# Transposing the softmax probabilities as 4-byte words of two keys in a cached attention kernel

## The chip, the cores and the metric

The kernel runs on one core of a Trainium2 chip. The metric is the device time of one execution in microseconds. Before the change, three runs took 957.71, 957.88 and 958.71 us, so the median is 957.88 us.

## The reference

There are two independent attention blocks, A and B, with weights and caches of their own. All inputs are bf16. For one block:

```python
B, Sq, D = 16, 64, 640
H, Sk, Dh = 32, 512, 128
q = (x @ wq).reshape(B, Sq, H, Dh).transpose(0, 2, 1, 3)
scores = einsum("bhqd,bhkd->bhqk", q, k_cache) * Dh ** -0.5
p = softmax(scores, axis=-1)
o = einsum("bhqk,bhkd->bhqd", p, v_cache)
out = o.transpose(0, 2, 1, 3).reshape(B, Sq, H * Dh) @ wo
```

The two outputs, each 16 x 64 x 640, are concatenated along the last axis. For each block, batch and head, the caches hold 512 keys and values of 128 numbers.

## The kernel before

**Tiling.** Two batches of 64 queries each share the 128 partitions. A *step* is one head of such a pair of batches, and a *macro step* `m` is two neighbouring heads (called `sub` 0 and 1 below). A pass goes through half of the heads (16) of one block for all eight pairs of batches. That makes 4 passes, 32 groups of 8 macro steps, and 256 macro steps in all. In a group the output projection is accumulated in PSUM over 16 heads. The first half's sum is parked in SBUF in f32 (OVP, ScalarE), and the second half's is added to it and stored (OVF, VectorE, then ST, a DMA that ScalarE issues).

**One macro step**, by the names in the code and the lines of the profile:

- KX (L433, TensorE): eight transposes of 128x128 blocks of K for one batch of the pair, into the one PSUM bank `KT_BANK`. KE (L442, VectorE) copies the bank to `ktp_ring`. Each is done twice a macro step, as KX0, KE0, KX1, KE1, and all four use the same bank.
- QP2 (L451, TensorE): the query projection, ten matmuls. QE2 (L459, ScalarE) copies it out with the scale.
- SM2 (L467, TensorE): the scores, four matmuls of 64 queries by 512 keys; two at a time share the array by its column halves.
- MX (L476, VectorE): the row maximum. EX (L482, ScalarE): the exponential, with the row sum. RC2 (L488, VectorE): the reciprocal of the sums.
- NM (L496, GpSimd): P times the reciprocal, one instruction per head, from `p_ring` to `pn_ring`. It also puts the keys in another order, described below.
- TR2 (L505, TensorE): eight transposes of 128x128 blocks of P into `PT_BANK`. The block of data is the weight load (stationary), and the identity is the moving operand. TE2 (L512, VectorE) copies the bank to `pT_ring`.
- PV2 (L524, TensorE): P times V, sixteen matmuls; a block of V is stationary, and 64 columns of `pT_ring` move. OE2 (L532, ScalarE) copies it out.
- OP2 (L540, L545, TensorE): the output projection, a matmul of 512 columns and one of 128 for each head.
- Once a group: XT (L604, TensorE) and XE (L612, ScalarE) transpose x for the projection, through `PT_BANK` too.

**Order.** Each engine runs a fixed list. Templates give an engine's order within one turn of the loop, and the number behind a name says how many macro steps ahead it works:

```python
PE_T = (("TR2", 1), ("QP2", 4), ("KX", 4, 0), ("SM2", 3), ("PV2", 1), ("XT", 0), ("OP2", 0), ("KX", 4, 1))
ACT_T = (("QE2", 4), ("OE2", 1), ("XE", 0), ("EX", 3, 0), ("EX", 3, 1), ("OV", 0), ("ST", -1))
DVE_T = (("TE2", 1), ("RC2", 2), ("KE", 4, 0), ("MX", 3, 0), ("MX", 3, 1), ("KE", 4, 1), ("OVF", 0))
POOL_T = (("NM", 0, 0), ("NM", 0, 1))
```

So on TensorE a turn goes TR2, QP2, KX0, SM2, PV2, (XT), OP2, KX1, and then the next turn's TR2. Semaphore waits are worked out from reads and writes of the buffers (`build_plan`, `prune_waits`), and the first instruction of an operation carries the wait. SyncE issues all loads by a plan with due times: K and V come in chunks of four heads into rings of five.

**The order of the keys.** V lies with key 4p + t on partition p in slot t. K's partitions hold eight neighbouring keys each, so the transposed K, the scores and P have their 512 keys in the order (key mod 8, key div 8): position 64 i + pp is key 8 pp + i. For PV2 the transposed P must have keys 4p + t on partition p, so NM writes its result permuted: with i = 4 th + tl, the key goes to place 128 tl + 2 pp + th.

Of the kernel before, what the change touches and what calls it, by code (L numbers as in the profile page):

```python
# [14 lines left out]
class Cfg:  # L15
    G = 4
    HH = 16
    NKB = 5
# [46 lines left out]
def build_plan(dims, cfg):  # L65
# [32 lines left out]
    def make_op(kind, m, sub):  # L98
        g0, g1 = 2 * m, 2 * m + 1
        ps_, bp, grp, h0 = step_info(g0)  # L100
        c = g0 // G
        if kind == "KX":
            return mk("pe", "KX", (m, sub), [("kn", c % cfg.NKB, g0 % G), ("kn", c % cfg.NKB, g1 % G), ("ident",)],
                      [("KTB",)], "KX%d" % sub, m, sub)
        if kind == "KE":
            return mk("dve", "KE", (m, sub), [], [("KTB",), ("ktp", m % cfg.NKT, sub)], "KE%d" % sub, m, sub)
        if kind in ("MX", "EX", "NM"):
            g = 2 * m + sub
            r = g % cfg.NR
            if kind == "MX":  # L110
                return mk("dve", "MX", g, [], [("SB", sub), ("negmax", r)], "MX%d" % sub, m, sub)
            if kind == "EX":
                return mk("act", "EX", g, [("negmax", r)], [("SB", sub), ("p", g % cfg.NP), ("rowsum", r)],
                          "EX%d" % sub, m, sub)
            return mk("pool", "NM", g, [("p", g % cfg.NP), ("recip", r)], [("pn", g % cfg.NPN)], "NM%d" % sub, m, sub)
        r0, r1 = g0 % cfg.NR, g1 % cfg.NR
        if kind in ("XT", "XE"):
            mt = m + cfg.XLEAD
            if mt % MPG != 0 or not (0 <= mt < NMAC):
                return None  # L120
            gq = mt // MPG
            m_ts = mt - cfg.XLEAD + OFF["TR2"]
            if kind == "XT":
                return mk("pe", "XT", gq, [("xn", gq % cfg.NXN), ("ident",)], [("PTB",)], "XT", m_ts, aux=gq)
            return mk("act", "XE", gq, [], [("PTB",), ("xT", gq % cfg.NX)], "XE", m_ts, aux=gq)
        if kind == "QP2":
            return mk("pe", "QP2", m, [("xT", grp % cfg.NX), ("wq", ps_ % 2, h0 // G)], [("QB",)], "QP2", m)
        if kind == "QE2":
            return mk("act", "QE2", m, [], [("QB",), ("qT", m % cfg.NQ)], "QE2", m)
        if kind == "SM2":  # L130
            return mk("pe", "SM2", m, [("qT", m % cfg.NQ), ("ktp", m % cfg.NKT, 0), ("ktp", m % cfg.NKT, 1)],
                      [("SB", 0), ("SB", 1)], "SM2", m)
        if kind == "RC2":
            return mk("dve", "RC2", m, [("rowsum", r0), ("rowsum", r1)], [("recip", r0), ("recip", r1)], "RC2", m)
        if kind == "TR2":
            return mk("pe", "TR2", m, [("pn", g0 % cfg.NPN), ("pn", g1 % cfg.NPN), ("ident",)], [("PTB",)], "TR2", m)
        if kind == "TE2":
            return mk("dve", "TE2", m, [], [("PTB",), ("pT", m % cfg.NT)], "TE2", m)
        if kind == "PV2":
            return mk("pe", "PV2", m, [("pT", m % cfg.NT), ("v", c % cfg.NVB, g0 % G), ("v", c % cfg.NVB, g1 % G)],  # L140
                      [("OB",)], "PV2", m)
        if kind == "OE2":
            return mk("act", "OE2", m, [], [("OB",), ("oT", m % cfg.NO)], "OE2", m)
        if kind == "OP2":
            return mk("pe", "OP2", m, [("oT", m % cfg.NO), ("wo", ps_ % 2, h0 // G)], [("OUTB",)], "OP2", m)
        if kind in ("OV", "OVF", "ST"):
            if h0 + 1 != SPB - 1:
                return None
            last_half = ps_ % NHALF == NHALF - 1
            if kind == "OV":  # L150
                if NHALF == 1:
                    return mk("act", "OV", m, [], [("OUTB",), ("out_sb", grp % 2)], "OV", m, aux=grp)
                if last_half:
                    return None
                return mk("act", "OVP", m, [], [("OUTB",), ("outp", bp)], "OV", m, aux=grp)
            if kind == "OVF":
                if NHALF == 1 or not last_half:
                    return None
                return mk("dve", "OVF", m, [("outp", bp)], [("OUTB",), ("out_sb", grp % 2)], "OV", m, aux=grp)
            if NHALF == 1 or not last_half:  # L160
                return None
            return mk("act", "ST", m, [("out_sb", grp % 2)], [("out_dram", grp)], "ST", m, aux=grp)
        raise ValueError(kind)

    templates = {"pe": cfg.PE_T, "dve": cfg.DVE_T, "pool": cfg.POOL_T, "act": cfg.ACT_T}
    for eng, tmpl in templates.items():
        offs = [t[1] for t in tmpl] + [cfg.XLEAD]
        for k in range(-max(offs), NMAC - min(offs)):
            for t in tmpl:
# [8 lines left out]
                if 0 <= m < NMAC:  # L178
                    op = make_op(kind, m, sub)
                    if op is not None:  # L180
                        progs[eng].append(op)
                        if op.kind == "OV":
                            progs[eng].append(mk("act", "ST", m, [("out_sb", op.aux % 2)], [("out_dram", op.aux)],
                                                 "ST", m, aux=op.aux))

    progs["pool"] = [mk("pool", "INIT1", -1, [], [("ones",)], "LDW", -10),
                     mk("pool", "INIT2", -1, [("ones",)], [("ident",)], "LDX", -10)] + progs["pool"]

    loads = []
    NEG = -10 ** 9  # L190
# [53 lines left out]
    def sem_key(op):  # L244
# [5 lines left out]
            return ("d_" + op.kind[2:].lower(), op.aux[0] % 2, op.aux[1])  # L250
        if op.kind == "ST":
            return ("d_out", op.aux % 2)
        if op.kind in ("INIT1", "INIT2"):
            return ("s_init",)
        return ("s_" + op.kind.lower(),)

# [90 lines left out]
def mha_kernel(nc, blocks, out, cfg=None):  # L347
# [30 lines left out]
    with contextlib.ExitStack() as es:  # L378
# [13 lines left out]
        qT_ring = sb("qT_ring", [128, NQ, 2, 128], BF16)  # L392
        p_ring = sb("p_ring", [128, NP, SK], BF16)
        pn_ring = sb("pn_ring", [128, NPN, SK], BF16)
        pT_ring = sb("pT_ring", [128, NT, 2, 4, 128], BF16)
        oT_ring = sb("oT_ring", [128, NO, 2, 128], BF16)
        out_sb = sb("out_sb", [128, 2, DN], BF16)
        negmax = sb("negmax", [128, NR], F32)
        rowsum = sb("rowsum", [128, NR], F32)
        recip = sb("recip", [128, NR], F32)  # L400
        ones_sb = sb("ones_sb", [128, 128], BF16)
        ident = sb("ident", [128, 128], BF16)
        ps = es.enter_context(nc.psum_tensor("ps", [128, 8, 512], F32))

        sems = {}
# [9 lines left out]
        S_BANK0 = 2  # L415
        PT_BANK, O_BANK, Q_BANK, KT_BANK = 4, 5, 6, 7
        pt_ps_flat = ps[:, PT_BANK, :].bitcast(BF16)
        pt_ps = pt_ps_flat.rearrange("p (s t q) -> p s t q", s=2, t=4)
        o_ps = ps[:, O_BANK, 0:256]
        q_ps = ps[:, Q_BANK, 0:256]  # L420
        kt_ps_flat = ps[:, KT_BANK, :].bitcast(BF16)
# [5 lines left out]
        def em_KX(e, op):  # L427
# [2 lines left out]
            c, hp = g0 // G, (g0 % G) // 2  # L430
            first = last = None
            for t8 in range(8):
                ins = e.transpose(kt_ps[:, t8, :], kn_ring[:, c % NKB, j, hp, t8, :], ident[:, :])  # L433
                first = first or ins
                last = ins
            return first, last
# [54 lines left out]
        def em_NM(e, op):  # L491
            g = op.idx
            r = g % NR
            src = p_ring[:, g % NP, :].rearrange("q (th tl pp) -> q th tl pp", th=2, tl=4)
            dst = pn_ring[:, g % NPN, :].rearrange("q (tl pp th) -> q th tl pp", tl=4, th=2)
            ins = e.tensor_scalar(dst, src, recip[:, r:r + 1], 1.0, ALU.mult, ALU.mult)  # L496
            return ins, ins

        def em_TR2(e, op):
            m = op.idx  # L500
            first = last = None
            for sub in range(2):
                g = 2 * m + sub
                for t in range(4):
                    ins = e.transpose(pt_ps[:, sub, t, :], pn_ring[:, g % NPN, t * 128:(t + 1) * 128], ident[:, :])  # L505
                    first = first or ins
                    last = ins
            return first, last

        def em_TE2(e, op):  # L510
            m = op.idx
            ins = e.tensor_copy(pT_ring[:, m % NT].rearrange("p s t q -> p (s t q)"), pt_ps_flat)  # L512
            return ins, ins

        def em_PV2(e, op):
            m = op.idx
            first = last = None
            for sub in range(2):
                g = 2 * m + sub
                c, gi = g // G, g % G  # L520
                for j in range(2):
                    for t in range(4):
                        col = sub * 128 + 64 * j
                        ins = e.matmul(o_ps[:, col:col + 64], v_ring[:, c % NVB, j, gi, t, :],  # L524
                                       pT_ring[:, m % NT, sub, t, 64 * j:64 * j + 64], start=(t == 0), stop=(t == 3))
                        first = first or ins
                        last = ins
            return first, last
# [18 lines left out]
            return first, last  # L547

        def em_OV(e, op):
            ins = e.activation(out_sb[:, op.aux % 2, :], out_ps_all, ACTF.Copy)  # L550
            return ins, ins

        def em_OVP(e, op):
# [3 lines left out]

        def em_OVF(e, op):
            blk, bp = grp_info(op.aux)
            ins = e.tensor_tensor(out_sb[:, op.aux % 2, :], out_ps_all, outp[:, bp, :], ALU.add)  # L560
            return ins, ins

        def em_ST(e, op):
            blk, bp = grp_info(op.aux)
            dst = out[2 * bp:2 * bp + 2, :, blk * DN:(blk + 1) * DN].rearrange("b q n -> (b q) n")
            ins = e.dma_start(dst, out_sb[:, op.aux % 2, :])
            return ins, ins

        def em_INIT1(e, op):
# [3 lines left out]
        def em_INIT2(e, op):  # L573
            ins = e.affine_select(ident[:, :], ones_sb[:, :], [[1, 128]], ALU.is_equal, 0.0, base=0,
                                  channel_multiplier=-1)
            return ins, ins

        def em_LDWQ(e, op):
# [37 lines left out]
        def em_LDKV(e, op):  # L616
# [6 lines left out]
            else:  # L623
# [4 lines left out]

        emitters = dict(KX=em_KX, KE=em_KE, QP2=em_QP2, QE2=em_QE2, SM2=em_SM2, MX=em_MX, EX=em_EX, RC2=em_RC2,
                        NM=em_NM, TR2=em_TR2, TE2=em_TE2, PV2=em_PV2, OE2=em_OE2, OP2=em_OP2, OV=em_OV,  # L630
                        OVP=em_OVP, OVF=em_OVF, ST=em_ST, XT=em_XT, XE=em_XE, INIT1=em_INIT1, INIT2=em_INIT2,
                        LDWQ=em_LDWQ, LDWO=em_LDWO, LDX=em_LDX, LDK=em_LDKV, LDV=em_LDKV)

        def run_program(e, prog, final_waits=()):
# [85 lines left out]
```

## Time and profile before

| | us |
|---|---|
| median of three runs | 957.88 |
| lowest, highest | 957.71, 958.71 |
| span of the profiled execution | 956.8 |
| TensorE busy (matmuls) | 919.4 |
| VectorE busy | 841.9 |
| ScalarE busy | 567.1 |
| GpSimd busy | 416.9 |

The profiled execution is one of its kind; its span runs from the first to the last recorded instruction. Its own time outside the span is not recorded, but the three runs are 0.9 to 1.9 us over its span, and the median is 1.1 over it. TensorE's granted clock is full from the first tenths of the span to the end (mean 0.998). DMA moves 299.5 MB, at 313 GB/s on average.

How to read it: busy time counts an instruction from start to end, and neighbouring instructions on one engine overlap, so the mean time of one matmul (219 ns for a 128x128 one) is longer than what it costs in a row of them. The chain of waits goes back from the last instruction and gives each stretch of time to one piece of work; there the overlap is taken out. "PE" is TensorE's matmuls, "PEld" its weight loads, "DVE" VectorE, "ACT" ScalarE, "POOL" GpSimd. The number after "L" is the line in the code. A shape such as `128*64 128x512` on a matmul is the stationary block (rows by columns) and then the moving operand; a name such as `ps<-ident,pn_ring` gives the output, the moving and the stationary operand.

### The profile page before, as it was taken

The page shows a single profiled execution, that of the slowest core. Times are in us where ns is not written, and L with a number is a line of the kernel's source. Part 1 is how long each engine was busy: PE and PEld are TensorE (multiplying, and loading weights), DVE is VectorE, ACT ScalarE, POOL GpSimd, SP SyncE. Part 2 cuts the span into 40 slices and gives each one's busy share as a digit, 9 for nine tenths or more (in the row PEclk, how much of TensorE's full clock was granted, in tenths as well). Part 3 has the DMA queues.
Part 4 walks back from the last instruction along what each step waited for, and adds up shares of the span by engine and source line. Part 5 has one row for each costly group of instructions (what it writes and reads, how often), then busy time and mean ns, then how long its engine had stood idle before and what let it go on. Part 6 is the DMA issues. An engine that isn't in the chain of part 4 may idle for free.

```text
span 956.8 us, 34351 instructions
## 1 busy us (share of the span) xinstructions
PE 919.4 (96%) x14755; PEld 733.5 (77%) x15008; DVE 841.9 (88%) x1552; ACT 567.1 (59%) x1585; POOL 416.9 (44%) x518
## 2 busy tenths in 40 slices
PE   4999999999999999999999999999999999999997
PEld 3877777778777777877777787777877778777775
DVE  2898899898899999899999899889899998999996
ACT  1666656666665565656566666666666656565654
POOL 0444444444444444444444444444444444444443
PEclk9999999999999999999999999999999999999999
DMA  9999999999999999888999999988888988899830
GB/s 315 364 365 364 351 365 367 365 368 351 338 337 337 343 330 315 299 292 305 322 332 352 326 353 327 306 294 296 302 305 288 308 301 297 295 297 314 295 124 15
DMA packets 230871, 299.51 MB, mean 313 GB/s; under 512 B 9536, under 2 KB 165184, under 8 KB 230720
## 3 DMA queue, kind: packets, MB, share of 16 engines
q1 hardware_dynamic: 228416, 294.69, 91.0%
q8 instruction: 118, 1.93, 0.8%
q10 hardware_dynamic: 2304, 2.62, 0.8%
q14 instruction: 33, 0.27, 0.1%
HBM read 294.65 MB, written 2.62 MB: 311 GB/s over the span
## 4 chain that ended last, share of the span: by engine, by line
PE 89%; DVE 4%; POOL 3%; issue 2%; SPq 1%; DMA 1%; POOLq 0%; DVEq 0%
PE ps L433 22%; PE ps L524 14%; PE ps L451 14%; PE ps L467 14%; PE ps L505 12%; PE ps L545 7%; PE ps L540 5%; POOL pn_ring L496 3%; DVE out_sb L560 1%; DVE ktp_ring L442 1%; DVE pT_ring L512 1%; PE ps L604 1%; DMA xn_ring<-in_A_x_dram 1%; SPq L626 1%; SPq L583 1%
## 5 line engine op out<-in xcount | busy, mean ns | idle before, releaser
L496 POOL TENSOR_SCALAR pn_ring<-p_ring,recip 128x512 bf16<-128x512 bf16 x512 | 416.3, 843 | 532.7 <-DVE recip L488 532.7
L442 DVE COPY ktp_ring<-ps 128x1024 bf16<-128x1024 bf16 x512 | 353.7, 691 | 105.3 <-PE ps L433 85.1
L482 ACT ACTIVATE p_ring<-ps,negmax 128x512 bf16<-128x512 f32 x512 | 345.6, 684 | 4.8 <-DVE negmax L476 4.8
L476 DVE TENSOR_REDUCE negmax<-ps 128x1 f32<-128x512 f32 x512 | 327.3, 681 | 0.4 <-PE ps L467 0.3
L433 PE MATMUL ps<-ident,kn_ring 128*128 128x128 bf16 x4096 | 314.6, 220 | 2.8 <-DMA kn_ring<-in_A_k_cache_dram 1.6
L532 ACT ACTIVATE oT_ring<-ps 128x256 bf16<-128x256 f32 x256 | 98.0, 383 | 306.0 <-PE ps L524 306.0
L433 PEld LDWEIGHTS ps<-ident,kn_ring 128*128 128x128 bf16 x4096 | 251.9, 98 | 34.2 <-DVE ktp_ring L442 2.6
L524 PEld LDWEIGHTS ps<-pT_ring,v_ring 128*128 128x128 bf16 x4096 | 133.5, 98 | 109.2 <-issue 100.0
L451 PE MATMUL ps<-xT_ring,wq_sb 128*128 128x128 bf16 x2560 | 186.4, 220 | 3.2 <-DMA wq_sb<-in_A_wq_dram 3.2
L512 DVE COPY pT_ring<-ps 128x1024 bf16<-128x1024 bf16 x256 | 174.5, 682 | 4.6 <-PE ps L505 3.8
L524 PE MATMUL ps<-pT_ring,v_ring 128*128 128x64 bf16 x4096 | 163.8, 194 | 3.3 <-issue 1.7
L467 PE MATMUL ps<-ktp_ring,qT_ring 128*64 128x512 bf16 x1024 | 159.8, 392 | 0.4 <-ACT p_ring L482 0.4
L505 PE MATMUL ps<-ident,pn_ring 128*128 128x128 bf16 x2048 | 156.7, 219 | 3.5 <-POOL pn_ring L496 3.5
L451 PEld LDWEIGHTS ps<-xT_ring,wq_sb 128*128 128x128 bf16 x2560 | 155.2, 98 | 3.5 <-DMA wq_sb<-in_A_wq_dram 3.5
L459 ACT ACTIVATE qT_ring<-ps 128x256 bf16<-128x256 f32 x256 | 98.4, 384 | 66.8 <-PE ps L451 66.8
L505 PEld LDWEIGHTS ps<-ident,pn_ring 128*128 128x128 bf16 x2048 | 124.1, 98 | 7.0 <-POOL pn_ring L496 6.7
L545 PE MATMUL ps<-wo_sb,oT_ring 128*128 128x128 bf16 x512 | 112.1, 219 | 13.4
L482 ACT ACTIVATION_READ_ACCUMULATOR p_ring<-ps,negmax 128x1 f32 x512 | 105.0, 205 | 0.0
L540 PE MATMUL ps<-wo_sb,oT_ring 128*128 128x512 bf16 x259 | 97.8, 379 | 0.0
L540 PEld LDWEIGHTS ps<-wo_sb,oT_ring 128*128 128x128 bf16 x512 | 50.1, 98 | 30.6 <-ACT oT_ring L532 0.3
L467 PEld LDWEIGHTS ps<-ktp_ring,qT_ring 128*64 128x64 bf16 x1024 | 36.1, 108 | 27.1 <-ACT p_ring L482 0.6
L545 PEld LDWEIGHTS ps<-wo_sb,oT_ring 128*128 128x128 bf16 x512 | 50.1, 98 | 0.0
(13 smaller groups left out, 112.7 us busy)
## 6 DMA issues: line engine op xcount, KB each, us to landing
kn_ring<-in_A_k_cache_dram SPq DMA_DIRECT2D x128, 512.0 KB, 7.0
v_ring<-in_A_v_cache_dram SPq DMA_DIRECT2D x128, 512.0 KB, 7.2
kn_ring<-in_B_k_cache_dram SPq DMA_DIRECT2D x126, 512.0 KB, 4.8
v_ring<-in_B_v_cache_dram SPq DMA_DIRECT2D x126, 512.0 KB, 5.7
wq_sb<-in_A_wq_dram SPq DMA_DIRECT2D x8, 640.0 KB, 10.4
wo_sb<-in_A_wo_dram SPq DMA_DIRECT2D x8, 640.0 KB, 10.2
wq_sb<-in_B_wq_dram SPq DMA_DIRECT2D x8, 640.0 KB, 8.4
wo_sb<-in_B_wo_dram SPq DMA_DIRECT2D x8, 640.0 KB, 7.5
```

The lines of the kernel that those rows point to most:

```text
L433: ins = e.transpose(kt_ps[:, t8, :], kn_ring[:, c % NKB, j, hp, t8, :], ident[:, :])
L442: ins = e.tensor_copy(dst, src)
L451: ins = e.matmul(q_ps[:, sub * 128:(sub + 1) * 128], wq_sb[:, ps_ % 2, kt, hh * DH:(hh + 1) * DH], xT_ring[:, grp % NX, kt, :], start=(kt ...
L467: ins = e.matmul(s_bank(sub)[64 * j:64 * j + 64, :], qT_ring[:, m % NQ, sub, 64 * j:64 * j + 64], ktp_ring[:, m % NKT, sub, j, :], start=T ...
L476: ins = e.reduce_max(negmax[:, r:r + 1], s_bank(g % 2), axis=AX.X, negate=True)
L482: ins = e.activation(p_ring[:, g % NP, :], s_bank(g % 2), ACTF.Exp, bias=negmax[:, r:r + 1], scale=1.0, accum_out=rowsum[:, r:r + 1])
L496: ins = e.tensor_scalar(dst, src, recip[:, r:r + 1], 1.0, ALU.mult, ALU.mult)
L505: ins = e.transpose(pt_ps[:, sub, t, :], pn_ring[:, g % NPN, t * 128:(t + 1) * 128], ident[:, :])
L512: ins = e.tensor_copy(pT_ring[:, m % NT].rearrange("p s t q -> p (s t q)"), pt_ps_flat)
L524: ins = e.matmul(o_ps[:, col:col + 64], v_ring[:, c % NVB, j, gi, t, :], pT_ring[:, m % NT, sub, t, 64 * j:64 * j + 64], start=(t == 0), s ...
L540: ins = e.matmul(out_ps0, oT_ring[:, m % NO, sub, :], wo_sb[:, ps_ % 2, hh, 0:N0], start=(hh == 0), stop=(hh == SPB - 1))
L545: last = e.matmul(out_ps1, oT_ring[:, m % NO, sub, :], wo_sb[:, ps_ % 2, hh, N0:DN], start=(hh == 0), stop=(hh == SPB - 1))
```

## The change

P is transposed as 4-byte words, each a pair of neighbouring bf16 keys. `pn_ring` is read as f32, so a head has 256 words a query, and TR2 issues two transposes of 128x128 words for a head (four a macro step) with an f32 identity. `ident4`, the identity in f32, is made by one more GpSimd instruction at the start (INIT3). The bank is filled with the same number of bytes, and TE2 copies it as bf16 as it did.

For this the two keys of a word must end on one partition. NM therefore writes key place 256 a + 4 pp + 2 th + sl: the four keys of a partition lie in two words, a = 0 and 1. The instruction has the same 512 elements a partition; its output goes in steps of four elements (8 bytes) and runs of 64, where it went in steps of two (4 bytes) and runs of 256. KX puts its eight blocks into other slots of the bank, so that the source can be read in the matching order. `pT_ring` now has the two keys of a word next to each other, so PV2's moving operand takes every second element.

`out_sb` has one buffer in place of two: the OVF of a group now waits for the store of the group before it, instead of the one before that.

The core of the diff:

```diff
-            return mk("pe", "TR2", m, [("pn", g0 % cfg.NPN), ("pn", g1 % cfg.NPN), ("ident",)], [("PTB",)], "TR2", m)
+            return mk("pe", "TR2", m, [("pn", g0 % cfg.NPN), ("pn", g1 % cfg.NPN), ("ident4",)], [("PTB",)], "TR2", m)
...
-                return mk("dve", "OVF", m, [("outp", bp)], [("OUTB",), ("out_sb", grp % 2)], "OV", m, aux=grp)
+                return mk("dve", "OVF", m, [("outp", bp)], [("OUTB",), ("out_sb", 0)], "OV", m, aux=grp)
...
+                     mk("pool", "INIT3", -1, [("ident",)], [("ident4",)], "LDX", -9)] + progs["pool"]
...
-        pT_ring = sb("pT_ring", [128, NT, 2, 4, 128], BF16)
+        pT_ring = sb("pT_ring", [128, NT, 2, 2, 128, 2], BF16)
...
-        out_sb = sb("out_sb", [128, 2, DN], BF16)
+        out_sb = sb("out_sb", [128, 1, DN], BF16)
...
+        ident4 = sb("ident4", [128, 128], F32)
...
-        pt_ps = pt_ps_flat.rearrange("p (s t q) -> p s t q", s=2, t=4)
+        pt_ps = ps[:, PT_BANK, :].rearrange("p (s a q) -> p s a q", s=2, a=2)
...
             for t8 in range(8):
-                ins = e.transpose(kt_ps[:, t8, :], kn_ring[:, c % NKB, j, hp, t8, :], ident[:, :])
+                th, a, sl = t8 // 4, (t8 // 2) % 2, t8 % 2
+                ins = e.transpose(kt_ps[:, a * 4 + th * 2 + sl, :], kn_ring[:, c % NKB, j, hp, t8, :], ident[:, :])
...
-            src = p_ring[:, g % NP, :].rearrange("q (th tl pp) -> q th tl pp", th=2, tl=4)
-            dst = pn_ring[:, g % NPN, :].rearrange("q (tl pp th) -> q th tl pp", tl=4, th=2)
+            src = p_ring[:, g % NP, :].rearrange("q (a hs pp) -> q a hs pp", a=2, hs=4)
+            dst = pn_ring[:, g % NPN, :].rearrange("q (a pp hs) -> q a hs pp", a=2, hs=4)
             ins = e.tensor_scalar(dst, src, recip[:, r:r + 1], 1.0, ALU.mult, ALU.mult)
...
-                for t in range(4):
-                    ins = e.transpose(pt_ps[:, sub, t, :], pn_ring[:, g % NPN, t * 128:(t + 1) * 128], ident[:, :])
+                for a in range(2):
+                    ins = e.transpose(pt_ps[:, sub, a, :], pn_ring[:, g % NPN, a * 256:(a + 1) * 256].bitcast(F32),
+                                      ident4[:, :])
...
                         ins = e.matmul(o_ps[:, col:col + 64], v_ring[:, c % NVB, j, gi, t, :],
-                                       pT_ring[:, m % NT, sub, t, 64 * j:64 * j + 64], start=(t == 0), stop=(t == 3))
+                                       pT_ring[:, m % NT, sub, t // 2, 64 * j:64 * j + 64, t % 2], start=(t == 0), stop=(t == 3))
...
+        def em_INIT3(e, op):
+            ins = e.tensor_copy(ident4[:, :], ident[:, :])
+            return ins, ins
```

More of the change, by code (lines that the diff above doesn't have):

```diff
@@ L151, in make_op @@
                 if NHALF == 1:
-                    return mk("act", "OV", m, [], [("OUTB",), ("out_sb", grp % 2)], "OV", m, aux=grp)
+                    return mk("act", "OV", m, [], [("OUTB",), ("out_sb", 0)], "OV", m, aux=grp)
                 if last_half:
@@ L158, in make_op @@
                     return None
-                return mk("dve", "OVF", m, [("outp", bp)], [("OUTB",), ("out_sb", grp % 2)], "OV", m, aux=grp)
+                return mk("dve", "OVF", m, [("outp", bp)], [("OUTB",), ("out_sb", 0)], "OV", m, aux=grp)
             if NHALF == 1 or not last_half:
                 return None
-            return mk("act", "ST", m, [("out_sb", grp % 2)], [("out_dram", grp)], "ST", m, aux=grp)
+            return mk("act", "ST", m, [("out_sb", 0)], [("out_dram", grp)], "ST", m, aux=grp)
         raise ValueError(kind)
@@ L182, in build_plan @@
                         if op.kind == "OV":
-                            progs[eng].append(mk("act", "ST", m, [("out_sb", op.aux % 2)], [("out_dram", op.aux)],
+                            progs[eng].append(mk("act", "ST", m, [("out_sb", 0)], [("out_dram", op.aux)],
                                                  "ST", m, aux=op.aux))
     progs["pool"] = [mk("pool", "INIT1", -1, [], [("ones",)], "LDW", -10),
-                     mk("pool", "INIT2", -1, [("ones",)], [("ident",)], "LDX", -10)] + progs["pool"]
+                     mk("pool", "INIT2", -1, [("ones",)], [("ident",)], "LDX", -10),
+                     mk("pool", "INIT3", -1, [("ident",)], [("ident4",)], "LDX", -9)] + progs["pool"]
     loads = []
@@ L252, in sem_key @@
             return ("d_out", op.aux % 2)
-        if op.kind in ("INIT1", "INIT2"):
+        if op.kind in ("INIT1", "INIT2", "INIT3"):
             return ("s_init",)
@@ L511, in em_TE2 @@
             m = op.idx
-            ins = e.tensor_copy(pT_ring[:, m % NT].rearrange("p s t q -> p (s t q)"), pt_ps_flat)
+            ins = e.tensor_copy(pT_ring[:, m % NT].rearrange("p s a q r -> p (s a q r)"), pt_ps_flat)
             return ins, ins
@@ L549, in em_OV @@
         def em_OV(e, op):
-            ins = e.activation(out_sb[:, op.aux % 2, :], out_ps_all, ACTF.Copy)
+            ins = e.activation(out_sb[:, 0, :], out_ps_all, ACTF.Copy)
             return ins, ins
@@ L559, in em_OVF @@
             blk, bp = grp_info(op.aux)
-            ins = e.tensor_tensor(out_sb[:, op.aux % 2, :], out_ps_all, outp[:, bp, :], ALU.add)
+            ins = e.tensor_tensor(out_sb[:, 0, :], out_ps_all, outp[:, bp, :], ALU.add)
             return ins, ins
@@ L565, in em_ST @@
             dst = out[2 * bp:2 * bp + 2, :, blk * DN:(blk + 1) * DN].rearrange("b q n -> (b q) n")
-            ins = e.dma_start(dst, out_sb[:, op.aux % 2, :])
+            ins = e.dma_start(dst, out_sb[:, 0, :])
             return ins, ins
@@ L630, in mha_kernel @@
                         NM=em_NM, TR2=em_TR2, TE2=em_TE2, PV2=em_PV2, OE2=em_OE2, OP2=em_OP2, OV=em_OV,
-                        OVP=em_OVP, OVF=em_OVF, ST=em_ST, XT=em_XT, XE=em_XE, INIT1=em_INIT1, INIT2=em_INIT2,
+                        OVP=em_OVP, OVF=em_OVF, ST=em_ST, XT=em_XT, XE=em_XE, INIT1=em_INIT1, INIT2=em_INIT2, INIT3=em_INIT3,
                         LDWQ=em_LDWQ, LDWO=em_LDWO, LDX=em_LDX, LDK=em_LDKV, LDV=em_LDKV)
```

## The prediction

> **What bounds the kernel now.** I read the page first, then the chain of waits (whole and for one stretch), then the waits, then the timeline of one macro step (two heads, 256 of them in all).
>
> The page: TensorE is busy 96% of the span, and nearly the whole chain that ended last lies on it. L505 holds the transposes that the change replaces. L467 holds the only weight loads that are not full 128x128 ones.
>
> ```profile
> PE 919.4 (96%) x14755; PEld 733.5 (77%) x15008; DVE 841.9 (88%) x1552; ACT 567.1 (59%) x1585; POOL 416.9 (44%) x518
> PE 89%; DVE 4%; POOL 3%; issue 2%; SPq 1%; DMA 1%; POOLq 0%; DVEq 0%
> L496 POOL TENSOR_SCALAR pn_ring<-p_ring,recip 128x512 bf16<-128x512 bf16 x512 | 416.3, 843 | 532.7 <-DVE recip L488 532.7
> L505 PE MATMUL ps<-ident,pn_ring 128*128 128x128 bf16 x2048 | 156.7, 219 | 3.5 <-POOL pn_ring L496 3.5
> L505 PEld LDWEIGHTS ps<-ident,pn_ring 128*128 128x128 bf16 x2048 | 124.1, 98 | 7.0 <-POOL pn_ring L496 6.7
> L467 PEld LDWEIGHTS ps<-ktp_ring,qT_ring 128*64 128x64 bf16 x1024 | 36.1, 108 | 27.1 <-ACT p_ring L482 0.6
> ```
>
> The chain between 328 and 337 us (start, us, what) gives the price of each block on TensorE, without the pipeline's overlap:
>
> ```profile
> 328.52 0.45 PE ps L433 x8
> 328.97 0.45 PE ps L505 x8
> 329.42 0.56 PE ps L451 x10
> 329.97 0.45 PE ps L433 x8
> 330.42 0.55 PE ps L467 x4
> 330.97 0.57 PE ps L524 x16
> 331.55 0.05 issue
> 331.60 0.22 PE ps L545
> 331.82 0.22 PE ps L540
> ...
> 332.54 0.45 PE ps L505 x8
> ```
>
> From one L505 block to the next is 3.57 us, and nothing but TensorE fills it. The eight transposes (TR2) take 0.45, that is 56 ns each although one row lasts 219: loads and streams overlap.
>
> The waits say how near the other engines stand:
>
> ```profile
> DVE ktp_ring L442 <- PE ps L433: 85.1, 258, 11.2
> PEld ps L505 <- POOL pn_ring L496: 6.7, 17, 0.9
> PEld ps L433 <- DVE ktp_ring L442: 2.6, 4, 1.1
> ```
>
> Only 17 of 256 TR2 blocks wait for GpSimd, and the K transposes (L433) hardly ever wait for VectorE's copy of their single PSUM bank. But not waiting is not the same as having room, as the timeline shows:
>
> ```profile
> 301.14 1.62 POOL L496 TENSOR_SCALAR pn_ring<-p_ring,recip 128x512 bf16<-128x512 bf16 x2 [1.94 <-DVE recip L488]
> 302.99 0.49 PEld L505 LDWEIGHTS ps<-ident,pn_ring 128*128 128x128 bf16 x8
> 303.25 0.69 DVE L442 COPY ktp_ring<-ps 128x1024 bf16<-128x1024 bf16 x1 [0.23 <-PE ps L433]
> 303.44 0.60 PEld L451 LDWEIGHTS ps<-xT_ring,wq_sb 128*128 128x128 bf16 x10
> 304.00 0.49 PEld L433 LDWEIGHTS ps<-ident,kn_ring 128*128 128x128 bf16 x8
> ```
>
> The copy KE1 ends at 303.25 + 0.69 = 303.94, and the next transposes KX0, which overwrite its bank, load at 304.00: 0.06 later. In the start-up, where KX0 really waited (29.93), it began 0.05 after the copy's end (29.20 + 0.68). The room is 0.01 us at most (4 ns in the unrounded rows). The bank's round trip, KX1, KE1, KX0, ties with the work between, KX1, TR2, QP2.
>
> **A shorter TR2 gains almost nothing.** KE1 starts when KX1 ends, before TR2, and does not move. If TR2 shrinks, KX0 waits at the bank instead; behind it in the queue stand SM2, PV2, OP2 and KX1, so the macro step stays 3.57. What can be gained: 0.004 in each of 239 macro steps (1.0 us), and the whole shortening in the 17 where TR2 came late. In one of those (321.66) KE1 ends at 322.26 and KX0 loads at 322.62, so 0.30 is free. A longer TR2, on the other hand, is paid in full, 256 times.
>
> **TR2: removed eight 2-byte transposes, added four 4-byte ones.** The trace has no 4-byte operand on TensorE. The lower bound is four at today's 56 ns, 0.22. The upper one is four passes over the data for each, 16 x 56 ns = 0.89, which nothing in the trace excludes. The nearest row by its weight load is L467, the only load of another form: 108 ns instead of 98 for half as many columns. There loads are not hidden: the block's four streams of 512 columns run as two pairs, the second 0.24 after the first (a block of 0.62, its last stream 0.379), while such a stream costs 0.22 with full loads (L540). So 64 columns add about 0.025, 128 about 0.05. Entering costs too: 0.55 for the block against 2 x 0.22 + 0.025 leaves 0.09. So does leaving: L524's 16 matmuls take 0.57, but their own spacing is (0.64 - 0.193) / 15 = 0.030, together 0.48, which leaves 0.09. With one pass and an unhidden load a transpose costs 0.056 + 0.05 = 0.106, four 0.42, with the entry 0.52. I take 0.52, because the form of the load is what visibly changes; the exit (0.61) I leave to the range, since half-width tiles are a second reason for it in L467. That is +0.07 a macro step: 256 x 0.07 = +18 us. Without entry cost: 0.42, about 1.4 us gained at most; with both +0.16, +41 us.
>
> The Trainium skill speaks on both sides here. TensorE: Matmul & The Clock Gate (Weight-path perf modes) says that the fast weight load is used only for 128 weights of a type other than FP32, and its LDWEIGHTS section puts a plain load at columns / 1.2 ns, 107 ns: by that, an estimate, four are 0.43 and the time stays at 957. The same page's Terms call the transpose mode 4x faster for FP32, which would make 0.22 likely. No row here shows either.
>
> **NM (GpSimd): same 512 elements, written in steps of 8 bytes in runs of 64, before in steps of 4 in runs of 256.** Bounds: 843 ns as now, or half as much again; below is excluded, since no element goes. I take 843, the row of the same operation and size. The pair ends at 302.76, TR2 loads at 302.99; at 321.66, where it waited, 0.06 after. So 0.17 of growth a pair is hidden. The Trainium skill, GPSIMD Engine Reference (Performance pitfalls for Q7 kernels), names a 50% penalty for reads in steps over 8 bytes; these are writes, just at 8, and no run here shows it.
>
> **PV2: its moving operand pT is now read every second element.** No row shows a strided stream. Bounds: nothing, or half rate, 16 x (0.0557 - 0.030) = 0.41 a macro step; a gain is excluded, as no column goes. I take nothing, since it has the same 64 columns and loads.
>
> **At no cost.** TE2 copies the same 128x1024 elements. KX writes the same eight tiles into other slots. INIT3 is one more GpSimd copy of 128x128 (the nearest, L574, took 0.29) while GpSimd idles until 18.4; the first TR2 is at 24.5. One out_sb buffer makes OVF on VectorE wait for the store of the group before: 8 steps or 29 us earlier, issued some 3 us after its OVF, landing in 5.6. Some 20 us cover it; without them TE2 would stand behind OVF, and PV2 behind that.
>
> **Sum.** The span is 956.8; the runs are 957.71 to 958.71, median 957.88, so about 1.1 lies around it. 957.9 + 18 = 976.
>
> **Rivals.**
> 1. Loads stay hidden, TR2 is 0.22: 17 x 0.22 = 3.8, with the 1.0 from the bank: 953. For: today's loads hide. Against: the load changes form. It decides where a 4-byte transpose stays below 0.445 / 4 = 111 ns; above that the kernel can't be faster.
> 2. No real halving: each 4-byte transpose is carried out as two of today's. TR2 stays 0.45, time 958.
> 3. Four passes: TR2 0.89, +0.45 x 256 = +115, 1073; more with entry and exit.
> 4. NM 50% slower: the ring TR2, TE2, RC2, NM becomes the bound. Where NM was late, TR2 at 321.66 led to NM at 323.18: 1.52 + 1.62 + 0.05 = 3.19; with 0.81 more 4.00, +0.43 a step: 1068.
> 5. PV2 at half rate: +0.41 x 256 = +105, 1063.
>
> **How the numbers follow.** Unhidden load 0.37 (976, own range 956 to 999), hidden 0.28 (953), no halving 0.10 (958), four passes 0.13, NM 0.06, PV2 0.06. Slower holds 0.60, so the forecast is slower. The range runs from 952, under the hidden case, to 1073, the four passes without extras; what is left out is four passes with drains, or two troubles together. Within 0.2% (1.9 us, about what a measurement of this kernel can tell from no change): no halving and the cheap end of the unhidden loads, 0.12. Faster 0.28.
>
> **What would show it.** Right: L505 at 4 x 256 streams, its block at about 0.5 in the chain, L496 at 843, L524 still 0.57, macro step 3.64, L433 not waiting for L442. Rival 1: L505 at 0.22 to 0.4, and L433 waiting for L442 nearly 256 times at a step of 3.57. Rival 3: the block near 0.9. Rival 4: L505 waiting for L496 in every step. Rival 5: L524 near 1.0. Wrong altogether: a macro step well under 3.57, which would mean that the bank doesn't hold KX0 back.

## The result and the profile after

The changed kernel takes 1127.72 us (1127.39 to 1128.87, four runs), against 958.30 for the kernel before in the same comparison: 1.177 times as long, with an interval of 1.175 to 1.178. That is 169 us slower. The direction is as forecast; the size is not (976 forecast, with a range up to 1073).

The page of the changed kernel. NM is now L499, TR2 L508, TE2 L516, PV2 L528, RC2 L491:

```profile
PE 984.2 (87%) x13984; PEld 742.2 (66%) x13984; DVE 865.8 (77%) x1552; ACT 569.5 (51%) x1585; POOL 683.1 (61%) x519
POOL 57%; PE 19%; DVE 18%; issue 4%; SPq 1%; DMA 1%; POOLq 0%; DVEq 0%
L499 POOL TENSOR_SCALAR pn_ring<-p_ring,recip 128x512 bf16<-128x512 bf16 x512 | 682.1, 1418 | 434.3 <-DVE recip L491 434.3
L508 PE MATMUL ps<-ident,pn_ring 128*128 128x128 f32 x1024 | 167.3, 286 | 122.7 <-POOL pn_ring L499 122.7
L508 PEld LDWEIGHTS ps<-ident,pn_ring 128*128 128x128 f32 x1024 | 107.8, 141 | 166.3 <-POOL pn_ring L499 153.0
```

The chain was 89% TensorE and is now 57% GpSimd. One NM takes 1418 ns where it took 843. But GpSimd is busy only 61% of the span, so it is not its throughput that binds. The waits of the changed kernel show 224 of 256 TR2 blocks waiting for NM (17 before), and TE2 then waiting for TR2:

```profile
PEld ps L508 <- POOL pn_ring L499: 153.0, 224, 1.9
DVE pT_ring L516 <- PE ps L508: 108.8, 240, 3.5
```

The chain of waits of the changed kernel, between 411 and 421 us, shows a ring: each pair of NM waits, through four other pieces of work, for the pair before it. It closes once a macro step (called a step from here on):

```profile
411.85 2.68 POOL pn_ring L499 x2
414.53 0.04 issue
414.58 0.67 PE ps L508 x4
415.25 0.02 issue
415.27 0.69 DVE pT_ring L516
415.96 0.08 DVE recip L491
416.04 0.08 issue
416.13 2.68 POOL pn_ring L499 x2
```

NM, TR2, TE2, RC2 and the next NM follow each other without a gap: 416.13 - 411.85 = 4.28 us, against 3.57 for a step in the undisturbed flow before. RC2 needs nothing of TE2. It stands behind it in VectorE's list, and that alone ties the next step's NM to this one's transposes in this ring. Over all 255 steps the mean from TR2 to TR2 is 4.29 us, against 3.63 before; 0.66 x 256 = 169 us, the whole loss.

### The profile page after: what moved, and what is told of

It is laid out like the page before. It is cut to its first block, busy times and chain, and to the rows that moved or that the text cites. A ratio compares the mean times of both kernels' runs of the same rounds, so it can differ in the third digit from the quotient of the medians.

```text
span 1125.6 us, 32557 instructions
## 1 busy us (share of the span) xinstructions
PE 984.2 (87%) x13984; PEld 742.2 (66%) x13984; DVE 865.8 (77%) x1552; ACT 569.5 (51%) x1585; POOL 683.1 (61%) x519
## 4 chain that ended last, share of the span: by engine, by line
POOL 57%; PE 19%; DVE 18%; issue 4%; SPq 1%; DMA 1%; POOLq 0%; DVEq 0%
POOL pn_ring L499 57%; DVE pT_ring L516 14%; PE ps L508 14%; DVE recip L491 2%; PE ps L436 1%; DVE out_sb L564 1%; DVE ktp_ring L445 1%; PE ps L454 1%; PE ps L528 1%; PE ps L470 1%; DMA xn_ring<-in_A_x_dram 1%; PE ps L544 1%; SPq L634 0%; SPq L591 0%; SPq L630 0%
## 5 line engine op out<-in xcount | busy, mean ns | idle before, releaser
L499 POOL TENSOR_SCALAR pn_ring<-p_ring,recip 128x512 bf16<-128x512 bf16 x512 | 682.1, 1418 | 434.3 <-DVE recip L491 434.3
L485 ACT ACTIVATE p_ring<-ps,negmax 128x512 bf16<-128x512 f32 x512 | 345.8, 685 | 1.8 <-DVE negmax L479 1.8
L508 PE MATMUL ps<-ident,pn_ring 128*128 128x128 f32 x1024 | 167.3, 286 | 122.7 <-POOL pn_ring L499 122.7
L516 DVE COPY pT_ring<-ps 128x1024 bf16<-128x1024 bf16 x256 | 177.0, 691 | 108.8 <-PE ps L508 108.8
L536 ACT ACTIVATE oT_ring<-ps 128x256 bf16<-128x256 f32 x256 | 98.3, 384 | 312.0 <-PE ps L528 312.0
L508 PEld LDWEIGHTS ps<-ident,pn_ring 128*128 128x128 f32 x1024 | 107.8, 141 | 166.3 <-POOL pn_ring L499 153.0
L528 PEld LDWEIGHTS ps<-pT_ring,v_ring 128*128 128x128 bf16 x4096 | 135.9, 97 | 107.4 <-issue 106.7
L454 PEld LDWEIGHTS ps<-xT_ring,wq_sb 128*128 128x128 bf16 x2560 | 165.7, 98 | 5.8 <-DMA wq_sb<-in_A_wq_dram 2.9
L528 PE MATMUL ps<-pT_ring,v_ring 128*128 128x64 bf16 x4096 | 166.4, 193 | 1.9 <-issue 1.7
L544 PE MATMUL ps<-wo_sb,oT_ring 128*128 128x512 bf16 x512 | 166.9, 380 | 0.0
L485 ACT ACTIVATION_READ_ACCUMULATOR p_ring<-ps,negmax 128x1 f32 x512 | 105.5, 206 | 0.0
```

The source lines that it names most:

```text
L454: ins = e.matmul(q_ps[:, sub * 128:(sub + 1) * 128], wq_sb[:, ps_ % 2, kt, hh * DH:(hh + 1) * DH], xT_ring[:, grp % NX, kt, :], start=(kt ...
L485: ins = e.activation(p_ring[:, g % NP, :], s_bank(g % 2), ACTF.Exp, bias=negmax[:, r:r + 1], scale=1.0, accum_out=rowsum[:, r:r + 1])
L508: ins = e.transpose(pt_ps[:, sub, a, :], pn_ring[:, g % NPN, a * 256:(a + 1) * 256].bitcast(F32), ident4[:, :])
L516: ins = e.tensor_copy(pT_ring[:, m % NT].rearrange("p s a q r -> p (s a q r)"), pt_ps_flat)
L544: ins = e.matmul(out_ps0, oT_ring[:, m % NO, sub, :], wo_sb[:, ps_ % 2, hh, 0:N0], start=(hh == 0), stop=(hh == SPB - 1))
```

## The experiments

Theory 1: NM's new write pattern, through the ring, is the whole loss. Theory 2: the 4-byte transposes cost a good part by themselves. The first four runs separate them and test what the prediction said of the K transposes' bank.

**Old NM pattern in the changed kernel** (the keys reach PV2 misplaced):

```diff
-            src = p_ring[:, g % NP, :].rearrange("q (a hs pp) -> q a hs pp", a=2, hs=4)
-            dst = pn_ring[:, g % NPN, :].rearrange("q (a pp hs) -> q a hs pp", a=2, hs=4)
+            src = p_ring[:, g % NP, :].rearrange("q (th tl pp) -> q th tl pp", th=2, tl=4)
+            dst = pn_ring[:, g % NPN, :].rearrange("q (tl pp th) -> q th tl pp", tl=4, th=2)
```

> The changed kernel with one thing undone: NM writes in the old pattern again (steps of 4 bytes, runs of 256), so the keys reach PV2 in a wrong order; all else is the change, the 4-byte transposes and PV2's strided operand included. Theory 1 (the whole loss is NM's 1418 ns, which makes the ring TR2, TE2, RC2, NM the bound): NM back to 843 ns, no wait for GpSimd in most macro steps, step about 3.6 us, 956 to 970 us; what is over 958 is the price of four 4-byte transposes at 109 ns with their entry (0.44 to 0.49 us against 0.45). Theory 2 (the 4-byte transposes cost a good part by themselves, through their longer latency): well over 980 us.

Measured: 961.66 us, 1.0033 (1.0021 to 1.0044) of the kernel before. NM is back at 844 ns, TR2 waits for it 17 times as before the change, and the median step is 3.574 us:

```profile
L499 POOL TENSOR_SCALAR pn_ring<-p_ring,recip 128x512 bf16<-128x512 bf16 x512 | 416.9, 844 | 534.5 <-DVE recip L491 534.5
PEld ps L508 <- POOL pn_ring L499: 6.6, 17, 0.9
```

All that remains of the change costs about 3 us, so theory 2 falls. From the last matmul before TR2 to the first after it, the starts lie 499 ns apart, against 503 in the kernel before: half as many transposes take the same time, 109 ns each where the 2-byte ones took 56. PV2's sixteen matmuls spread over 459 ns from first start to last, against 447: the strided operand costs 12 ns a step.

**New NM pattern in the kernel before** (the same two lines the other way; the keys reach PV2 misplaced):

> The kernel before with one part of the change alone: NM writes in the new pattern (steps of 8 bytes, runs of 64), so the keys reach PV2 in a wrong order; transposes and all else as before. Theory 1 (NM alone): NM about 1418 ns, the ring is TR2 0.65 + TE2 0.59 + RC2 0.25 + NM 2.67 + 0.05 = 4.2 us, so 958 + 256 x 0.65 = 1120 to 1130 us. Theory 2 (the 4-byte transposes cost a good part): clearly below the changed kernel's 1128 us, 1050 to 1100.

Measured: 1118.63 us, 1.167 (1.165 to 1.169). This one edit makes 160 of the 169 us. Its median step is 4.225 us, where the sum gave 4.2. The other 9 go with the longer latency of the 4-byte transposes: their block counts 0.67 in the ring, where the bf16 one counts 0.63 in this run, and 256 x 0.04 = 10 us.

```profile
411.43 0.63 PE ps L505 x8
```

**RC2 ahead of TE2 in the changed kernel:**

```diff
-    DVE_T = (("TE2", 1), ("RC2", 2), ("KE", 4, 0), ("MX", 3, 0), ("MX", 3, 1), ("KE", 4, 1), ("OVF", 0))
+    DVE_T = (("RC2", 2), ("TE2", 1), ("KE", 4, 0), ("MX", 3, 0), ("MX", 3, 1), ("KE", 4, 1), ("OVF", 0))
```

> The changed kernel, with VectorE's order changed: RC2 stands ahead of TE2, so that the reciprocals and NM no longer wait for this turn's transposes. NM keeps its 1418 ns. If the loss is the latency of the ring and not GpSimd's throughput (2.67 of 4.27 us busy), the ring is now SM2, MX, EX, RC2, NM, TR2, and RC2 can start at the end of EX: 1.0 us after TR2's start in the trace of before, so 1.0 + 0.25 + 2.67 + 0.05 = 3.97 us a step, 1060 us. If GpSimd's throughput were the bound: no change, 1128 us.

Measured: 1017.20 us, 1.061 (1.060 to 1.063). The order of two VectorE instructions, with NM as slow as before, takes 110 us off: latency, not throughput. It is 43 us better than my sum, which named the wrong ring. The steps are not 3.97 but of two kinds that mostly alternate, 3.62 and 3.93, with a mean of 3.85 over all. The chain of this run shows what binds (OE2 is L536 here, EX L485; the dots leave out lines):

```profile
399.44 2.67 POOL pn_ring L499 x2
...
402.15 0.66 PE ps L508 x4
...
404.37 0.60 PE ps L528 x16
...
404.99 0.38 ACT oT_ring L536
405.37 1.34 ACT p_ring L485 x4
...
406.74 0.18 DVE recip L491
...
407.00 2.67 POOL pn_ring L499 x2
```

NM is followed by TR2, PV2, OE2, EX, RC2 and NM again: EX stands behind OE2 in ScalarE's list, and OE2 waits for PV2. This ring closes once in two steps, after 407.00 - 399.44 = 7.56 us, a long and a short one together, so 3.78 for each.

**Half of TR2 in the kernel before** (four transposes a macro step; what is left out keeps old data):

```diff
-                for t in range(4):
+                for t in range(4 if m < 1 else 2):
```

> The kernel before with TR2 cut to four transposes in each macro step but the first (half of P is not transposed anew): 0.22 us instead of 0.45 for the block. Theory (the K transposes' PSUM bank ties, so KX0 waits for KE1): 953 us, L433 waits for L442 in nearly every macro step, step still 3.57 us. Rival (TensorE's busy time is the bound): 958 - 256 x 0.22 = 901 us.

Measured: 945.04 us, 0.986 (0.985 to 0.987). The bank does hold KX0 back: this run's waits show `L433` waiting for `L442` 240 times, and of the 57 us by which TR2 got shorter, 13 arrive in the time. That is more than the 4.8 I allowed, for the step fell by 44 ns to 3.523. This run's waits and timeline show why:

```profile
PEld ps L433 <- DVE ktp_ring L442: 44.2, 240, 1.1
407.55 0.69 DVE L442 COPY ktp_ring<-ps 128x1024 bf16<-128x1024 bf16 x1 [0.23 <-PE ps L433]
408.30 0.45 PEld L433 LDWEIGHTS ps<-ident,kn_ring 128*128 128x128 bf16 x8 [0.18 <-DVE ktp_ring L442]
408.30 0.62 PE L433 MATMUL ps<-ident,kn_ring 128*128 128x128 bf16 x8
```

The load that waits starts 0.06 after the copy's end, as I had said, but the first matmul starts with it (408.30 both). In the undisturbed flow of the kernel before, the load ran 0.05 ahead of its matmul (304.00 and 304.05). That lead was room that I had not counted.

The other runs ask what in NM's pattern is slow, what a 4-byte transpose's 109 ns are, and whether the loss can be undone with NM as it is.

**Eight patterns of NM in the kernel before,** one a macro step in turn. The keys are misplaced.

```diff
+            k = (g // 2) % 8
...
+            elif k == 4:  # write step 8 B, runs of 64 (as the change)
+                ins = e.tensor_scalar(N.rearrange("q (x b r) -> q x r b", x=2, r=4),
+                                      P.rearrange("q (x r b) -> q x r b", x=2, r=4), sc, 1.0, ALU.mult, ALU.mult)
...
```

Each `k` has a line of its own, so that the profile tells them apart:

| line | write | read |
|---|---|---|
| L497 | flat | flat |
| L499 | step 4 B, runs of 256 | flat |
| L502 | step 4 B, runs of 64 | flat |
| L505 | step 8 B, runs of 128 | flat |
| L508 | step 8 B, runs of 64 | flat |
| L511 | step 16 B, runs of 64 | flat |
| L514 | flat | step 128 B, runs of 4 |
| L517 | flat | step 8 B, runs of 128 |

> The kernel before, with NM's access pattern changed from macro step to macro step in turn (eight patterns, a line of code each, always the same 512 elements); the keys are misplaced. Read the mean ns of each line. Theory 1 (the step of the write counts): about 843 for flat writes and steps of 4 bytes, with runs of 256 or of 64 alike; about 1418 for steps of 8 bytes, with runs of 128 or 64 alike; as much or more for 16 bytes. Theory 2 (short runs count): 64-element runs in steps of 4 bytes cost far over 843, and runs of 128 in steps of 8 bytes less than 1418. Flat writes with strided reads: if reads are charged like writes, about 1418 for reads in steps of 8 bytes, more for 128 bytes.

Its groups on GpSimd in one profiled execution, each 64 instructions of 512 elements (the last number before the second bar is the mean ns):

```profile
L511 POOL TENSOR_SCALAR pn_ring<-p_ring,recip 128x512 bf16<-128x512 bf16 x64 | 154.3, 2601 | 50.3 <-DVE recip L488 50.3
L508 POOL TENSOR_SCALAR pn_ring<-p_ring,recip 128x512 bf16<-128x512 bf16 x64 | 84.9, 1410 | 50.3 <-DVE recip L488 50.3
L505 POOL TENSOR_SCALAR pn_ring<-p_ring,recip 128x512 bf16<-128x512 bf16 x64 | 84.8, 1408 | 56.5 <-DVE recip L488 56.5
L514 POOL TENSOR_SCALAR pn_ring<-p_ring,recip 128x512 bf16<-128x512 bf16 x64 | 72.4, 1144 | 57.0 <-DVE recip L488 57.0
L499 POOL TENSOR_SCALAR pn_ring<-p_ring,recip 128x512 bf16<-128x512 bf16 x64 | 52.0, 843 | 84.0 <-DVE recip L488 84.0
L502 POOL TENSOR_SCALAR pn_ring<-p_ring,recip 128x512 bf16<-128x512 bf16 x64 | 52.0, 841 | 74.2 <-DVE recip L488 74.2
L517 POOL TENSOR_SCALAR pn_ring<-p_ring,recip 128x512 bf16<-128x512 bf16 x64 | 45.6, 726 | 66.3 <-DVE recip L488 66.3
L497 POOL TENSOR_SCALAR pn_ring<-p_ring,recip 128x512 bf16<-128x512 bf16 x64 | 43.5, 692 | 85.0 <-DVE recip L488 85.0
```

The step of the write counts, and the length of the run does not: 841 and 843 at 4 bytes, 1408 and 1410 at 8, 2601 at 16, with 2 ns of difference by the run. Strided reads cost less: 726 in steps of 8 bytes, and 1144 in steps of 128, against 692 flat.

**4-byte transposes cut down, in the changed kernel with the old NM pattern:**

```diff
+                    W = pn_ring[:, g % NPN, a * 256:(a + 1) * 256].bitcast(F32)
+                    if m % 3 == 0:
+                        ins = e.transpose(pt_ps[:, sub, a, :], W, ident4[:, :])
+                    elif m % 3 == 1:
+                        ins = e.transpose(pt_ps[:, sub, a, 0:64], W[0:64, :], ident4[0:64, 0:64])
+                    else:
+                        ins = e.transpose(pt_ps[0:64, sub, a, :], W[:, 0:64], ident4[:, :])
```

> The changed kernel with NM's old pattern, and the 4-byte transposes cut down in turn from macro step to macro step: whole (128 words loaded, 128 identity columns streamed), half the stream (64 rows of queries, so 64 identity columns, still 128 columns loaded), half the load (64 words loaded, 128 columns streamed). What is not transposed anew is left as it was. Read the spacing of the four matmuls, 109 ns when whole. Theory 1 (the load is what isn't hidden: 56 + 53): half the stream 80 to 109, half the load about 82. Theory 2 (a 4-byte operand streams at half rate, loads hidden): half the stream about 55, half the load 109. Theory 3 (loads alone, hidden stream): half the stream 109, half the load 55.

The three forms have the lines L510 (whole), L512 (half the stream) and L514 (half the load). Three blocks from the timeline (start, us of the four together):

```profile
400.05 0.46 PE L512 MATMUL ps<-ident,pn_ring 64*128 64x64 f32 x4
403.86 0.60 PE L514 MATMUL ps<-ident,pn_ring 128*64 128x128 f32 x4
407.43 0.61 PE L510 MATMUL ps<-ident,pn_ring 128*128 128x128 f32 x4
```

One matmul of L510 and of L514 lasts 273 ns, so their spacing is (0.61 - 0.273) / 3 and (0.60 - 0.273) / 3, both 0.11: half the load saves nothing. Of L512 one lasts 223 ns, so its mean spacing is 0.08; the single starts are 111 ns apart at first and then 62 and 63. So the load is hidden, and my unhidden load is refuted. What sets the 109 ns is then most likely the stream, at about half the rate of a 2-byte operand. (With 2-byte operands and all 128 rows loaded, 64 columns in place of 128 bring the spacing from 56 ns to 30, in PV2.) L512 can't show this alone, for it halves the stationary rows together with the stream, and its block with the gaps to its neighbours (540 ns from the last matmul before to the first after) is longer than a whole one (499). Whether the 62, rather than 55, is already the load's own limit stays open too.

**The transposes one macro step later, in the changed kernel:**

```diff
-    NPN = 3
+    NPN = 4
-    XLEAD = 10
+    XLEAD = 9
-    PE_T = (("TR2", 1), ("QP2", 4), ("KX", 4, 0), ("SM2", 3), ("PV2", 1), ("XT", 0), ("OP2", 0), ("KX", 4, 1))
-    ACT_T = (("QE2", 4), ("OE2", 1), ("XE", 0), ("EX", 3, 0), ("EX", 3, 1), ("OV", 0), ("ST", -1))
-    DVE_T = (("TE2", 1), ("RC2", 2), ("KE", 4, 0), ("MX", 3, 0), ("MX", 3, 1), ("KE", 4, 1), ("OVF", 0))
+    PE_T = (("TR2", 0), ("QP2", 4), ("KX", 4, 0), ("SM2", 3), ("PV2", 0), ("XT", 0), ("OP2", -1), ("KX", 4, 1))
+    ACT_T = (("QE2", 4), ("OE2", 0), ("XE", 0), ("EX", 3, 0), ("EX", 3, 1), ("OV", -1), ("ST", -2))
+    DVE_T = (("TE2", 0), ("RC2", 2), ("KE", 4, 0), ("MX", 3, 0), ("MX", 3, 1), ("KE", 4, 1), ("OVF", -1))
...
-        ones_sb = sb("ones_sb", [128, 128], BF16)
+        ones_sb = ident4[:, 0:64].bitcast(BF16)
```

> The changed kernel with TR2, TE2, PV2, OE2, OP2 and what follows moved one macro step later against RC2 and NM (and one more pair of buffers less one for pn_ring; the scratch of the identity shares a buffer). NM keeps its pattern and its 1418 ns. If the loss is latency alone (NM's time in a ring that closes within one step), GpSimd's 2.7 us fit into a step of 3.6 and the time falls to 954 to 966 us, near that of the changed kernel with the old pattern. If NM's slow writes also hold up others (VectorE or the DMA, through the memory): over 980 us.

Measured: 953.44 us, 0.9945 (0.9932 to 0.9957), just under the expected range. The changed kernel is 174 us faster by this edit and half a percent faster than the kernel before, with NM as slow as ever:

```profile
L499 POOL TENSOR_SCALAR pn_ring<-p_ring,recip 128x512 bf16<-128x512 bf16 x512 | 684.6, 1421 | 258.9 <-DVE recip L491 258.9
```

No wait for NM is left on TensorE in this run. GpSimd is busy 72% of the span, and its slow writes hold up nothing else.

**Controls in the kernel before.** First RC2 ahead of TE2, the edit shown above:

> The kernel before with RC2 ahead of TE2 in VectorE's order, nothing else. Control for the same edit on the changed kernel, and a candidate to beat both. NM is far from the bound here, so the regular step stays 3.57 us. In the 16 macro steps after an OVF, NM comes some 0.6 us earlier, so TR2's wait of 0.33 goes, but PV2's wait for TE2 grows by RC2's 0.15: 954 to 958 us. If the order costs something in regular steps (TE2 held up by EX through RC2): over 960.

Measured: 955.73 us, 0.9973 (0.9963 to 0.9983), as expected. Then the later place of the transposes, the edit shown above with one `out_sb`:

> The kernel before, bf16 transposes and old NM pattern, with the same later place for TR2, TE2, PV2, OE2 and OP2 as in the run before (and one buffer for out_sb, four for pn_ring). It asks whether the change itself has any part in that run's 953.4 us. Theory (the gain over 958 is all the later place, which takes TR2's waits for NM after each OVF away, and the 4-byte transposes save nothing): 950 to 954 us, no slower than that run. If the 4-byte transposes do save: over 955.

Measured: 951.10 us, 0.9920 (0.9906 to 0.9933), the best of all. It keeps the 2-byte transposes, so the later place explains the gain, and the 4-byte ones make it about 2 us smaller, near the 3 us that they and PV2's strided operand cost in the first run.

**NM's loops turned in the changed kernel** (same result, flat writes):

```diff
-            src = p_ring[:, g % NP, :].rearrange("q (a hs pp) -> q a hs pp", a=2, hs=4)
-            dst = pn_ring[:, g % NPN, :].rearrange("q (a pp hs) -> q a hs pp", a=2, hs=4)
+            src = p_ring[:, g % NP, :].rearrange("q (a hs pp) -> q a pp hs", a=2, hs=4)
+            dst = pn_ring[:, g % NPN, :].rearrange("q (a pp hs) -> q a pp hs", a=2, hs=4)
```

> The changed kernel, with the loops of NM's access pattern turned: the same keys go to the same places, but the writes run flat and the reads jump by 128 bytes in runs of 4. In the run of eight patterns this took 1144 ns, against 1410 for the change's own. If the ring TR2, TE2, RC2, NM is the bound, its step falls from 4.27 by 2 x 0.27 less what the pair overlaps, to 3.75 to 3.85 us: 990 to 1025 us. If only patterns at 843 ns helped, nothing changes.

Measured: 1037.74 us, 1.082 (1.081 to 1.084). The ring is confirmed, but I missed the size: the pair takes 2.30 us, two full NM of 1156 ns with no overlap, where I had counted on some (the pair of the changed kernel takes 2.68, less than 2 x 1418). The median step is 3.89.

## Why the prediction was wrong

- **The step that failed is NM's price.** "I take 843, the row of the same operation and size" was wrong: it was 1418. The row had the size, but not the write step, which is what counts. The upper bound, half as much again, was wrong too. It rested on no row of the trace. The Trainium skill, GPSIMD Engine Reference (Performance pitfalls for Q7 kernels), has that figure for reads in steps over 8 bytes; here writes in steps of 8 cost 68% more than in steps of 4, reads in steps of 8 only 5% more than flat ones (726 against 692), and reads in steps of 128, in runs of four, 65% more (1144).
- **Rival 4 was the right mechanism, mis-sized and held too unlikely.** It named the ring with a step of 4.00 us and 1068 us. Measured were 4.28 and 1127.7. Of the 0.28 us between, 0.25 is the pair of NM (2.68 against 1.62 + 0.81 = 2.43); the rest is the longer block of 4-byte transposes (0.67 against 0.62) less small change in the other terms. With a bound of twice the time for NM the same ring would have given 1.52 + 3.24 + 0.05 = 4.81, and a range that held the result. The price decided from 0.17 us a pair on; it was 1.06.
- **TR2's single transpose had nearly the right number, by luck.** 0.106 was forecast and 0.109 measured, but the unhidden load behind it is refuted. The entry cost of 0.09 does not exist either (first spacing 115 against 109), and the terms given, 0.42 and 0.09, add up to 0.51 and not 0.52. So TR2's block got 4 ns shorter where the forecast had it 70 longer, and the forecast's +18 us were about 3; PV2's 12 ns a step less TR2's 4 make 2 of them. The price was that of rival 2 (no halving, block unchanged, 958), held at 0.10: with the old NM pattern the time is 961.66. Of the two rules of the Trainium skill weighed there (TensorE: Matmul & The Clock Gate, LDWEIGHTS and Terms), the plain load at 107 ns gave the right spacing for a cause that the run with half the load excludes, and the 4x faster transpose mode did not bring a 4-byte transpose down to 56 ns.
- **The tie of the K transposes' bank held**, but with about 0.05 us more room than was counted: halving TR2 brought 13 us, not 57 and not 4.8.
- **PV2 at no cost** was right up to 12 ns a step. INIT3 (0.29 us) and the single `out_sb` cost nothing that the waits show.

## What to carry to other kernels

Before a busy engine's work is made cheaper at the expense of an idle one, follow the idle one's result to who waits for it: at 44% busy GpSimd had 0.17 us of room, because an in-order list tied it into a ring. An access pattern is part of an instruction's price; a row of the same size in another pattern is not its price, and where no row has the pattern, the upper bound must be wide. A loss by latency can be cheap to undo by giving the late step one more turn, here 174 us for one more buffer of `pn_ring`, and that is worth trying on the kernel that is already fast: it brought 8 us there.

## What the runs showed of the hardware

- GpSimd's time for 512 bf16 elements grows with the write's step: 692 ns flat, 843 at 4 bytes, 1408 at 8, 2601 at 16. Strided reads cost less: 726 ns at 8 bytes, 1144 at 128.
- A 128x128 transpose of 4-byte words costs 109 ns in a row of them, and one of 2-byte words 56, so pairing keys in a word saved next to nothing on TensorE (499 ns for the block with its neighbours, against 503).
- The load of the K transposes ran 0.05 us ahead of its matmul, and that lead hid about as much of a wait: with the wait on every step, load and matmul started together, and the step was 44 ns shorter, not 4.
